# Attention and a two-layer block on one core: DMA transposes for one batch's q and k and another's x, and a reordered start

## The chip, the cores and the metric

The kernel runs on one core of a Trainium2 chip. The metric is device time in microseconds (us): the median of the runs shown, lower is better. A core has a matrix engine (PE; its weight loads, PEld, overlap the matmuls), a vector engine (DVE), a scalar engine (ACT), a general engine (POOL) and a sync engine (SP) that only issues DMAs here. Each engine takes its instructions strictly in the program's order and waits on semaphores for the others. ACT and POOL issue DMAs too, in line with their own work.

## The reference

Sliding-window causal attention over 8 batches, 8 heads, 576 positions, head size 64; its output, with the heads side by side, is the input x (4608 x 512) of a small two-layer block.

```python
scale = 1.0 / np.sqrt(D)
scores = scale * np.matmul(q, k.transpose(0, 1, 3, 2))
mask = (rel >= 0) & (rel < 64)              # rel = query position - key position
scores = np.where(mask, scores, -1e9)
attn = softmax(scores)
x = (attn @ v).transpose(0, 2, 1, 3).reshape(B * S, H * D)
h = x @ w_in                                # 512 -> 2048
g = h - np.tanh(h)
out = g @ w_out                             # 2048 -> 512, float32
```

## The kernel before

**Attention, by batch and pair of heads.** Heads r and r + 4 make a pair; g = 4 * batch + pair runs from 0 to 31. The 576 positions are nine windows of 64. For each pair q and k are loaded as rows, cast to bf16 (`cast`), transposed on PE in six pieces each against an identity (`tr`, L203) into PSUM, and copied to `qT` and `kT` (two buffers each, used in turn) by ACT or DVE. `qT` holds the two heads in separate halves of a zeroed tile, so one matmul per window gives both heads' scores (`scores`, L216), in three groups of three windows with one exponential on ACT each (L220). In batches 0 and 1 the mask is added by a second matmul (L219); later it is multiplied in by DVE (`masking`). `pv` (L230) multiplies by V with a column of ones, and `norm` divides on DVE into `xs`. For batches 0 to 2 the finished `xs` is transposed on PE (`x_tr`, L247) and copied out of PSUM into the chunk tiles `xT`; from batch 3 on, SP issues two DMA transposes straight from `xs` into `xT` (`x_dma`, L262).

**V.** V is loaded eight positions to a partition, moved into `vb` with the ones column in four pieces (`cast_v`), and spread by nine small DMAs (`keys_v`, L133) into the upper half of `vw`; the lower half is the same moved by one window (`shift_v`: DVE at L139 in batches 0 and 1, a DMA at L141 later). There is one `vb` and one V load tile, so a batch's V waits for the one before to be moved on.

**The two-layer block.** Nine chunks of 512 positions. The program runs in half steps h: at even h four matmuls (`hp_mm`, L273) make 128 columns of h for one chunk, ACT takes the tanh (L277), DVE subtracts (L283) into `gT`; at odd h four matmuls (`yp_mm`, L293) work on the output of the chunk before. One chunk takes 32 half steps; chunk c starts at h = 32c. `w_in` is loaded in three parts (512, 512 and 1024 columns: steps `w0`, `w1`, `w2`, needed at h = 0, 8 and 16), `w_out` in four (`o0` to `o3`).

**What sets the order.** Everything is placed by hand. Batches 0 to 2 are a script, `PLAN`, with an entry for a half step and an entry -1 for all that comes before the first; its letters are read by `play`: `q`/`r` load one pair's q/k, `Q`/`K`/`V` load a batch's q/k/v, `v` one pair's v, `a`/`b` cast q/k, `d` moves V into `vb`, `k` is a `keys_v` move, `z` the shift, `E`/`F` transpose q/k, `R` a group of scores, `P` a pair's `pv` and `norm`, `M` masking, `X` an x transpose, `w`/`o` weight loads, `i` the identity, `m` constants, `n` the mask; the last letters name the engine (p POOL, a ACT, v DVE, s SP). Batches 3 to 7 follow rules: pair g is transposed at half step a = 8g - 48 - (0, 2 or 4), scored at a + 5, a + 7 and a + 9, masked at a + 11, multiplied with V from a + 13, normalised at a + 15; loads and V's moves stand at fixed distances from s = 32b - (0, 2 or 4). For batch 7 that is a = 172, 180, 188, 196 and s = 220. From batch 4 on `pace` puts a tiny POOL copy that waits for a given step's `gT` ahead of each load, so that POOL doesn't issue it early.

SP issues, in program order, the `keys_v` moves, the shift, `x_dma` and the output rows (`y_out`); POOL issues all casting loads and does most casts.

Of the kernel before, what the change touches and what calls it, by code (L numbers as in the profile page):

```python
# [8 lines left out]
BF16 = mybir.dt.bfloat16  # L9
# [6 lines left out]
def kernel(  # L16
# [9 lines left out]
    nc = tc.nc  # L26
    B, H, S, D = q.shape
    NP = H // 2
    NJ = S // 64
    E, P = 6, S // 6  # L30
# [12 lines left out]
    const = ctx.enter_context(tc.tile_pool(name="const", bufs=1))  # L43
# [4 lines left out]
    sm_pool = ctx.enter_context(tc.tile_pool(name="sm", bufs=3))  # L48
    xt_pool = ctx.enter_context(tc.tile_pool(name="xt", bufs=3))
    g_pool = ctx.enter_context(tc.tile_pool(name="g", bufs=2))  # L50
    psum = ctx.enter_context(tc.tile_pool(name="psum", bufs=1, space=PSUM))


# [11 lines left out]
    NR, NPT = 2, 4  # L65
# [5 lines left out]
    PT = [const.tile([128, NJ, 128], BF16, name=f"pt{i}") for i in range(NPT)]  # L71
    kT = [const.tile([128, 64 + S], BF16, name=f"kt{i}") for i in range(NR)]
    qT = [const.tile([128, 2, S], BF16, name=f"qt{i}") for i in range(NR)]
    xs = [const.tile([128, NJ, NP, D], BF16, name=f"xs{i}") for i in range(2)]

    stage, rows, whole = {}, {}, {}
# [31 lines left out]
    def cast(g, n, eng=nc.gpsimd):  # L108
        t = row_pool.tile([P, E, 2, D], BF16, tag=n + "b", name=n + "b")
        move(eng, t.rearrange("p e h d -> p h e d"),  # L110
             stage.pop((g, n)).rearrange("p h (e d) -> p h e d", d=D))
        rows[g, n] = t

    def load_v(b, pr):
        if (b, "v") not in whole:
# [52 lines left out]
    def more_constants():  # L168
        nc.vector.memset(qT[1], 0.0)
        nc.vector.memset(kT[1][:, 0:64], 0.0)  # L170
        for i in range(2):
            nc.vector.memset(vw[i][0:64, 0], 0.0)

        for h in range(2):
            nc.gpsimd.memset(hide[:, h], 0.0)
            nc.gpsimd.affine_select(hide[:, h], hide[:, h], compare_op=ALU.is_ge, fill=-(2.0 ** 30),
                                    base=-1, pattern=[[-1, 64]], channel_multiplier=1)
            nc.gpsimd.affine_select(hide[:, h], hide[:, h], compare_op=ALU.is_ge, fill=-(2.0 ** 30),  # L180
                                    base=64, pattern=[[1, 64]], channel_multiplier=-1)

    def make_mask():
        nc.gpsimd.memset(seen, 1.0)
# [59 lines left out]
    def x_tr(b, half, w0, w1, bank, eng=nc.vector):  # L244
        tp = ps[:, bank, :].bitcast(BF16)[:, 0:640].rearrange("p (w t) -> p w t", t=128)
        for w in range(w0, w1):
            nc.tensor.transpose(tp[:, w - w0, :],  # L247
                                xs[b % 2][:, w, 2 * half:2 * half + 2, :].rearrange("p r d -> p (r d)"), ident)
        lo, hi = b * NJ + w0, b * NJ + w1
        while lo < hi:  # L250
            c = lo // WPC
            to = min(hi, (c + 1) * WPC)
            i0 = lo - b * NJ - w0
            move(eng, chunk_tile(c)[:, lo - c * WPC:to - c * WPC, half, :], tp[:, i0:i0 + to - lo])
            lo = to

    def x_dma(b):
        lo, hi = b * NJ, (b + 1) * NJ
        while lo < hi:
            c = lo // WPC  # L260
            to = min(hi, (c + 1) * WPC)
            nc.sync.dma_start(out=chunk_tile(c)[:, lo - c * WPC:to - c * WPC].rearrange("p w r t -> p (w r) t"),  # L262
                              in_=xs[b % 2][:, lo - b * NJ:to - b * NJ].rearrange("p w r d -> p (w r d)"),
                              transpose=True)
            lo = to
# [40 lines left out]
    def at(h, *fn):  # L306
        items.setdefault(h, []).append(fn)
# [8 lines left out]

    ENG = dict(p=nc.gpsimd, a=nc.scalar, v=nc.vector, s=nc.sync)

    def play(script):
        for step in script.split():
            what = step[0]
            n = [int(i, 36) for i in step[1:] if i not in "apvs"]
            eng = [ENG[i] for i in step[1:] if i in "apvs"]
            if what in "qr":
                load(*n, "q" if what == "q" else "k", *eng)
            elif what in "QK":
                load_all(*n, what.lower())
            elif what == "V":  # L330
                load_v_all(*n)
            elif what == "a":
                cast(*n, "q", *eng)
            elif what == "b":
                cast(*n, "k", *eng)
            elif what == "v":
                load_v(*n)
            elif what == "d":
                cast_v(*n, *eng)
            elif what == "k":  # L340
                keys_v(*n, *eng)
            elif what == "z":
                for j in (0, 4) if eng[0] is nc.vector else (0,):
                    shift_v(*n, j, j + 4 if eng[0] is nc.vector else NJ - 1, *eng)
            elif what == "E":
                tr(*n, "q", 3, *eng)
            elif what == "F":
                tr(*n, "k", 2 if n[0] < 2 * NP else 3, *eng)
            elif what == "R":
                scores(*n, (4, 0, 1)[n[1]] if n[0] < NP else 4)  # L350
            elif what == "P":
                for i in range(3):
                    pv(*n, i)
                norm(*n)
            elif what == "M":
                masking(*n)
            elif what == "X":
                b, half, part = n
                x_tr(b, half, 4 * part, 4 + 5 * part, 2 if part == 1 and b < 2 else 3, *eng)
            elif what == "w":  # L360
                load_w_in(*n)
            elif what == "o":
                load_w_out(*n)
            elif what == "i":
                make_ident()
            elif what == "n":
                make_mask()
            elif what == "m":
                more_constants()
# [1 line left out]

    PLAN = {
        -1: """
            v02 i q0a v00 a0v v01 d00a d02a d01v r2a m v03 q3p r1p d03p r0s q1a k03p k01a E0vv
            b0a k07p b2a q2p k00s b1v F0v k04p R01 V1 n k05s k02s k06a k08s R00 K1 a1v R02 Q1
            r3s E1vv w0 F1a F2a z0v R10 w1 a2p E2aa d12p d13a R11 R22 P0 d10a R12 R21 a3p d11p
            b3a E3aa k12s R20 P1 k13p F3v K2 a4p P2 k18s a7p k10s b7p Q2 k16s b4p w2 k11s R31
            R30 V2 a5p X000v a6p R32 P3 b6p o3 b5p X001a k15a X010v X011a o2 E4vv""",
        0: "a8p F4a",
        10: "R40 F5a b8p R42 b9p E5aa",  # L380
        12: "k14s R41 k17s z1v",
        15: """
            R50 a9p d21p E6av R51 F6v R52 P4 d23p R62 d22p bAa o1 F7v R61 d20p E7aa P5 R60 bBp
            o0""",
        16: "aAp R70 E8aa",
        20: "R72 X101a k23s X100v k21s k24s k27s P6",
        23: "F8a R71 F9a k22s P7 k25s k20s R80 k28p k26p E9av",
        24: "R82",
        27: "R81 z2s X110a",
        31: "R90 X111v M8 EAav",  # L390
        32: "R92",
        35: "FAa R91",
        36: "M9",
        41: "aBa P9 FBa",
        42: "RA1",
        45: "RA2 P8 EBaa RA0",
        50: "RB1 X201v RB2 MA X200a RB0 PA",
        56: "MB PB",
        60: "X210a",
        62: "X211a",  # L400
    }
    for h, script in PLAN.items():
        at(h, play, script)


    for g in range(3 * NP, B * NP):
        b, pr = divmod(g, NP)
        a = 8 * g - 48 - (0, 2, 4)[min(b - 3, 2)]
        s = 32 * b - (0, 2, 4)[min(b - 3, 2)]
        at(a - 7, cast, g, "q")  # L410
        at(a - 5, cast, g, "k")
        at(s - 72 + 5 * pr, cast_v, b, pr)
        at(a, tr, g, "q", 3, nc.scalar, nc.vector)
        at(a + 2, tr, g, "k", 3, nc.scalar)
        for i in range(3):
            at(a + 5 + 2 * i, scores, g, i, 4)
        at(a + 11, masking, g)
        for i in range(3):
            at(a + 13 + i, pv, g, i)
        at(a + 15, norm, g)  # L420
        if pr == NP - 1:
            at(a + 16, x_dma, b)
        for j in range(NJ):
            if pr == 0:
                at(s - 54 + j // 2, keys_v, b, j)
        if pr == 0:
            if b < 4:
                at(s - 78, load_v_all, b)
                at(s - 64, load_all, b, "q")
                at(s - 63, load_all, b, "k")  # L430
            else:
                for h, f in (s - 78, (load_v_all, b)), (s - 60, (load_all, b, "q")), (s - 64, (load_all, b, "k")):
                    at(h, pace, h)
                    at(h, *f)
            at(s - 47, shift_v, b, 0, NJ - 1)

    LAG = 16
    for h in range(min(items), 2 * (16 * NC + LAG) + 2):
        n = h // 2
# [42 lines left out]
```

## Time and profile before

| | |
|---|---|
| median of 5 runs | 353.88 us (351.64 to 354.59) |
| profiled execution, its own time | 354.85 us |
| its span (first to last instruction) | 353.1 us |
| first matmul of h = 0 | 40.47 us into the span |
| PE busy | 318.2 us, 90% |
| DVE, ACT, POOL busy | 203.2, 200.1, 106.7 us |
| mean granted PE clock | 0.995 |

"Busy" counts an engine's instructions from start to end; PE matmuls overlap, so the distance from one start to the next says more than their duration. In the lists below, a line of the timeline has the start, the time from the first start to the last end of its instructions, engine, source line, operation, what is written and read, and how many instructions; a bracket gives the idle time before it and what ended that. Issues of DMAs stand as work of the issuing queue (SPq, ACTq), on POOL as POOL's own.

### The profile page before, as it was taken

What the parts mean: (1) busy time and instruction counts of PE and PEld (TensorE: products, weight loads), DVE (VectorE), ACT (ScalarE), POOL (GpSimd) and SP (SyncE); (2) the same over time, 40 slices, a digit from 0 to 9 for tenths busy, and PEclk for the clock granted to TensorE, in tenths of its full rate; (3) what the DMA queues carried; (4) which work ended last, traced back from release to release, by engine and by line L of the source; (5) the groups of instructions that cost most, each with busy time, mean ns of one, the idle gap of its engine ahead of it and who ended that gap; (6) DMA issues with size and microseconds to landing.
All of it is one profiled execution on the core that took longest, in us unless ns stands there. A gap on an engine that the chain in (4) does not pass through costs nothing.

```text
span 353.1 us, 5838 instructions
## 1 busy us (share of the span) xinstructions
PE 318.2 (90%) x2208; PEld 184.5 (52%) x2239; DVE 203.2 (58%) x319; ACT 200.1 (57%) x360; POOL 106.7 (30%) x151
## 2 busy tenths in 40 slices
PE   0357778999899999999999999999999999999995
PEld 0347546655556555555555555555555444444442
DVE  2435568865676666666666767776676333334400
ACT  3446478965756666566566666666664444444411
POOL 6928526406407430832462246330000000000000
PEclk9999899999999999999999999999999999999999
DMA  7999993759864766976686678544001400010021
GB/s 141 179 196 211 219 192 55 151 99 178 176 125 68 133 109 143 161 138 117 115 160 135 133 148 128 126 101 97 32 31 40 119 30 32 30 59 32 30 84 66
DMA packets 43692, 39.85 MB, mean 113 GB/s; under 512 B 15408, under 2 KB 37552, under 8 KB 43280
## 3 DMA queue, kind: packets, MB, share of 16 engines
q0 software_dynamic: 20368, 18.02, 34.8%
q1 hardware_dynamic: 22456, 20.37, 21.4%
q10 hardware_dynamic: 840, 1.08, 1.1%
q8 instruction: 17, 0.28, 0.3%
q14 instruction: 11, 0.09, 0.1%
HBM read 36.70 MB, written 9.44 MB: 131 GB/s over the span
## 4 chain that ended last, share of the span: by engine, by line
PE 77%; DVE 7%; ACT 6%; DMA 3%; issue 1%; POOL 1%; ACTq 0%; POOLq 0%
PE ps L293 33%; PE ps L273 32%; PE ps L216 4%; PE ps L230 4%; DMA vall<-in_v_dram 3%; PE ps L203 3%; DVE xs L241 3%; DVE gT L283 2%; ACT pt L220 2%; ACT th L277 2%; ACT qt L80 1%; PE ps L219 1%; DVE qt L82 1%; DVE pt L224 1%; POOL vw L133 1%
## 5 line engine op out<-in xcount | busy, mean ns | idle before, releaser
L283 DVE TENSOR_TENSOR gT<-ps,th 128x512 bf16<-128x512 f32 x144 | 99.4, 692 | 91.7 <-ACT th L277 89.0
L273 PE MATMUL ps<-xT,wi 128*128 128x512 bf16 x576 | 148.5, 381 | 1.9 <-DVE gT L283 1.1
L293 PE MATMUL ps<-w_out_sb,gT 128*128 128x512 bf16 x545 | 140.1, 379 | 1.8 <-ACT ysb L298 0.2
L277 ACT ACTIVATE th<-ps 128x512 f32<-128x512 f32 x144 | 86.0, 598 | 79.3 <-PE ps L273 78.8
L273 PEld LDWEIGHTS <-wi 128*128 128x128 bf16 x576 | 61.1, 114 | 47.5 <-issue 3.6
L293 PEld LDWEIGHTS <-gT 128*128 128x128 bf16 x576 | 53.6, 98 | 53.8 <-issue 0.5
L220 ACT ACTIVATE pt<-ps 128x384 bf16<-128x384 f32 x96 | 47.0, 491 | 37.2 <-PE ps L216 29.9
L241 DVE TENSOR_TENSOR xs<-ps,rc 64x576 bf16<-64x576 f32 x64 | 48.3, 755 | 1.5
L82 POOL COPY vb<-vall 72x1024 bf16<-72x1024 bf16 x27 | 28.3, 1057 | 51.9 <-DMA vall<-in_v_dram 42.5
L216 PE MATMUL ps<-qt,kt 128*128 128x128 bf16 x288 | 37.5, 230 | 7.2 <-ACT pt L220 4.5
L82 POOL COPY qb<-qall 96x768 bf16<-96x768 bf16 x29 | 24.1, 832 | 38.4 <-DMA qall<-in_q_dram 27.8
L230 PE MATMUL ps<-vw,pt 128*128 128x130 bf16 x288 | 30.1, 229 | 4.6 <-DVE vw L139 2.0
L230 PEld LDWEIGHTS <-pt 128*128 128x128 bf16 x288 | 23.1, 103 | 20.0 <-issue 3.0
L82 DVE COPY qt<-ps 64x576 bf16<-64x576 bf16 x29 | 21.9, 757 | 16.9 <-ACT qt L80 13.6
L216 PEld LDWEIGHTS <-kt 128*128 128x128 bf16 x288 | 25.2, 104 | 11.0 <-DVE kt L82 2.2
L298 ACT ACTIVATE ysb<-ps 128x512 f32<-128x512 f32 x36 | 21.5, 598 | 14.7 <-PE ps L293 14.7
L82 POOL COPY kb<-kall 96x768 bf16<-96x768 bf16 x27 | 22.9, 847 | 9.9 <-PE ps L203 6.6
L80 ACT ACTIVATE qt<-ps 64x576 bf16<-64x576 bf16 x35 | 22.3, 637 | 0.9 <-PE ps L203 0.9
L203 PE MATMUL ps<-ident,kb 96*128 96x96 bf16 x192 | 14.6, 217 | 7.5 <-ACT kb L80 5.7
L203 PE MATMUL ps<-ident,qb 96*128 96x96 bf16 x192 | 14.7, 217 | 6.4 <-DVE qb L82 6.1
L80 ACT ACTIVATE kt<-ps 128x576 bf16<-128x576 bf16 x28 | 18.1, 648 | 2.7 <-PE ps L203 2.6
L203 PEld LDWEIGHTS <-kb 96*128 96x128 bf16 x192 | 12.3, 104 | 13.5 <-ACT kb L80 5.9
(49 smaller groups left out, 131.5 us busy)
## 6 DMA issues: line engine op xcount, KB each, us to landing
out_dram<-ysb SPq DMA_DIRECT2D x36, 256.0 KB
vw<-vb SPq DMA_DIRECT2D x63, 65.0 KB
vall<-in_v_dram POOLq DMA_DIRECT2D x7, 576.0 KB, 12.3
kall<-in_k_dram POOLq DMA_DIRECT2D x7, 576.0 KB, 6.9
qall<-in_q_dram POOLq DMA_DIRECT2D x7, 576.0 KB, 8.7
vw<-vw SPq DMA_DIRECT2D x6, 520.0 KB
w_out_sb<-in_moe_w_out_dram POOLq DMA_DIRECT2D x4, 512.0 KB, 10.9
wi<-in_moe_w_in_dram POOLq DMA_DIRECT2D x2, 512.0 KB, 19.1
```

Source lines behind the costliest of these rows:

```text
L80: nc.scalar.activation(o, i, ACT.Copy)
L82: eng.tensor_copy(o, i)
L203: nc.tensor.transpose(tp[:, e, :], src[:, e, :], ident[:P, :P])
L216: nc.tensor.matmul(sp[:, i, :], kT[g % NR][:, 64 * j:64 * j + 128], qT[g % NR][:, :, 64 * j:64 * j + 64], start=True, stop=g >= 2 * NP)
L220: nc.scalar.activation(PT[g % NPT][:, 3 * grp:3 * grp + 3, :], sp, ACT.Exp, scale=scale)
L230: nc.tensor.matmul(ps[:, 5 + grp, 130 * i:130 * i + 130], PT[g % NPT][:, j, :], vw[b % 2][:, j, 2 * pr:2 * pr + 2, :], start=True, stop=True)
L241: nc.vector.tensor_tensor(xo[r, :, :, pr, :], ov[r, :, :, h, 0:D], rc[r].to_broadcast([64, 3, 3, 64]), ALU.mult)
L273: nc.tensor.matmul(hp, w_in_tile(ki, m), chunk_tile(c)[:, :, ki % 2, 64 * (ki // 2):64 * (ki // 2) + 64], start=(ki == 0), stop=(ki == 3))
L277: nc.scalar.activation(th, hp, ACT.Tanh)
L283: nc.vector.tensor_tensor(gT[c][:, m, :], hp, th, ALU.subtract)
L293: nc.tensor.matmul(yp, gT[c][:, m, s * 128:(s + 1) * 128], w_out_sb[:, m, :], start=(m == 0), stop=(m == M - 1))
L298: nc.scalar.activation(ysb, ps[:, yp_bank(c, s), :], ACT.Copy)
```

## The change

```diff
+    dram = ctx.enter_context(tc.tile_pool(name="dram", bufs=2, space=bass.MemoryType.DRAM))
+    qz = [const.tile([P, 2, E, 128], BF16, name=f"qz{i}") for i in range(2)]
...
+    def cast_q(g):
+        i = stage.pop((g, "q")).rearrange("p h (e d) -> p h e d", d=D)
+        for h in range(2):
+            nc.gpsimd.tensor_copy(qz[g % 2][:, h, :, 64 * h:64 * h + 64], i[:, h])
+
+    def bounce(g, n):
+        if n == "q":
+            t = dram.tile([2, S, 128], BF16, tag="q", name="qd")
+            nc.sync.dma_start(out=t.rearrange("h (p e) c -> p h (e c)", e=E),
+                              in_=qz[g % 2].rearrange("p h e c -> p h (e c)"))
+        else:
+            t = dram.tile([S, 128], BF16, tag="k", name="kd")
+            nc.sync.dma_start(out=t.rearrange("(p e) c -> p (e c)", e=E),
+                              in_=rows.pop((g, "k")).rearrange("p e h d -> p (e h d)"))
+        rows[g, n + "d"] = t
+
+    def tr_dma(g, n):
+        t = rows.pop((g, n + "d"))
+        if n == "q":
+            nc.sync.dma_start(out=qT[g % NR].rearrange("c h s -> c (h s)"),
+                              in_=t.rearrange("h s c -> (h s) c"), transpose=True)
+        else:
+            nc.sync.dma_start(out=kT[g % NR][:, 64:], in_=t, transpose=True)
...
+            elif what == "Y":
+                x_dma(*n)
...
     PLAN = {
         -1: """
-            v02 i q0a v00 a0v v01 d00a d02a d01v r2a m v03 q3p r1p d03p r0s q1a k03p k01a E0vv
-            b0a k07p b2a q2p k00s b1v F0v k04p R01 V1 n k05s k02s k06a k08s R00 K1 a1v R02 Q1
-            r3s E1vv w0 F1a F2a z0v R10 w1 a2p E2aa d12p d13a R11 R22 P0 d10a R12 R21 a3p d11p
-            b3a E3aa k12s R20 P1 k13p F3v K2 a4p P2 k18s a7p k10s b7p Q2 k16s b4p w2 k11s R31
-            R30 V2 a5p X000v a6p R32 P3 b6p o3 b5p X001a k15a X010v X011a o2 E4vv""",
+            r2a q0s v02 v03 v00 v01 a0v r0s d00a d01v d02a m i r1p q3p q1a d03p b0a k01s a1v
+            k08s k00s b1p k03p n k02s F0a E0av R01 R02 q2p E1av k07p V1 k06a a3p k04p b2v K1 a2a
+            R00 F1v k05s r3a E2aa F2a Q1 w0 R10 z0v d12p R22 d13p R12 P0 R11 E3aa R20 P1 d10p
+            b3a d11p k12s k13p R21 k16p a7p w1 F3a b4a P2 a4p R30 R31 X000v Q2 R32 P3 b7a X001a
+            k10s K2 b5p a6p F4a k18s w2 X010v k11s k17s b6p a5p b9p V2 k15a X011v E4vv""",
...
-        50: "RB1 X201v RB2 MA X200a RB0 PA",
+        50: "MA RB2 RB0 PA RB1",
         56: "MB PB",
-        60: "X210a",
-        62: "X211a",
+        58: "Y2",
     }
...
+    def more_zeros(i):
+        nc.gpsimd.memset(qz[i], 0.0)
...
+    for i in range(2):
+        at(66 + 2 * i, more_zeros, i)
...
-        at(a - 7, cast, g, "q")
-        at(a - 5, cast, g, "k")
         at(s - 72 + 5 * pr, cast_v, b, pr)
-        at(a, tr, g, "q", 3, nc.scalar, nc.vector)
-        at(a + 2, tr, g, "k", 3, nc.scalar)
+        if b < 7:
+            at(a - 7, cast, g, "q")
+            at(a, tr, g, "q", 3, nc.scalar, nc.vector)
+        else:
+            at(a - 14, cast_q, g)
+            at(a - 12, bounce, g, "q")
+            at(a - 6, tr_dma, g, "q")
+        if b < 7:
+            at(a - 5, cast, g, "k")
+            at(a + 2, tr, g, "k", 3, nc.scalar)
+        else:
+            at(a - 13, cast, g, "k")
+            at(a - 11, bounce, g, "k")
+            at(a - 5, tr_dma, g, "k")
...
-                for h, f in (s - 78, (load_v_all, b)), (s - 60, (load_all, b, "q")), (s - 64, (load_all, b, "k")):
+                hq, hk = s - (60 if b < 7 else 68), s - (64 if b < 7 else 72)
+                for h, f in (s - 78, (load_v_all, b)), (hq, (load_all, b, "q")), (hk, (load_all, b, "k")):
```

The entries of `PLAN` for h = 0 to 45 are reordered in the same way. Of those that the prediction speaks of: F4 goes from h = 0 into the start, F5 from ACT to DVE, F7 from DVE to ACT, and R40 from h = 10 to 15. In batch 7 q and k of a pair now go from POOL's cast to a DRAM tile (two DMAs) and from there by two DMA transposes into `qT` and `kT`; q's rows carry zeros in the other head's half, so the transposes write the whole of `qT`. Batch 2's x goes by `x_dma` at h = 58 in place of eighteen PE transposes.

## The prediction
> **What bounds the kernel now.** I read the page's 40 slices first, then PE's timeline in the steady part, then the chain of waits and the engines' timelines in the first 41 us.
>
> ```profile
> PE   0357778999899999999999999999999999999995
> DMA  7999993759864766976686678544001400010021
> L203 PE MATMUL ps<-ident,kb 96*128 96x96 bf16 x192 | 14.6, 217 | 7.5 <-ACT kb L80 5.7
> ```
>
> PE is full from about 90 us to the end, and starved for the first 40, where the DMA engines are full instead. So a PE instruction taken out late is worth its whole step, one taken out early little, and the start is a matter of what arrives when. One transpose has a mean of 217 ns, but its step must be read from starts:
>
> ```profile
> 239.68 0.41 PE L203 MATMUL ps<-ident,kb 96*128 96x96 bf16 x6
> 239.94 1.03 PE L293 MATMUL ps<-w_out_sb,gT 128*128 128x512 bf16 x4
> 240.80 1.03 PE L273 MATMUL ps<-xT,wi 128*128 128x512 bf16 x4
> ...
> 249.25 1.03 PE L273 MATMUL ps<-xT,wi 128*128 128x512 bf16 x4
> ```
>
> Six 96-column transposes hold PE 239.94 - 239.68 = 0.26 us. A pair's eight half steps take 249.25 - 240.80 = 8.45 us with no idle bracket; the same eight without attention take 293.76 - 286.85 = 6.91 us later in that timeline.
>
> **The change, last batch.** Out: per pair 12 transposes. 4 pairs x 2 x 0.26 = 2.08 us of full PE, plus three copies per pair (ACT 0.63 and 0.65, DVE 0.76) on engines that are 60 to 70% busy there. Call it -2.0. The DMA work that replaces it is hidden if it is in time, and two queues decide that.
>
> POOL first. These are its rows for batch 7 now:
>
> ```profile
> 207.21 1.05 POOL L82 COPY vb<-vall 72x1024 bf16<-72x1024 bf16 x1 [6.80 <-DMA vall<-in_v_dram]
> ...
> 216.44 0.77 POOL L99 DMA_DIRECT2D qall<-in_q_dram  x1 [0.30 <-issue]
> ...
> 226.08 0.83 POOL L82 COPY qb<-qall 96x768 bf16<-96x768 bf16 x1 [7.80 <-DMA qall<-in_q_dram]
> ```
>
> The q load moves from h = 160 to 152 (by 8.45 us), but it stands behind the V copy that ends at 208.2, a k load and two casts (0.78 + 0.84 + 0.83), two paced copies and their gaps (about 0.9): issue near 211.6, not 208. Landing took 9.5 us from issue here, 6.1 for k: 217.7 to 221.1. Behind the new `cast_q` of pair 28, which waits for it, stand one V copy and the cast of k of pair 27: 0.83 (two halves of one cast) + 1.05 + 0.83 = 2.7, so k of pair 27 is ready at 220.4 to 223.8. PE transposes it at 222.78 now. Loss 0 to 1.0; I take 0.5.
>
> SP second. Per pair it gains two writes (0.53 each by the shift's row) and two DMA transposes. A transpose costs SP 1.18 to 1.57 us to issue (L262, 2 to 16 blocks), and for q and k I take 1.4 and 1.3. Four pairs: 4 x 3.8 = 15 us in 30 us of an SP that now issues about 11 us there, and each transpose waits for its write. The transposes of pair 28 and V's nine moves (0.65 each) share SP from h = 166: by adding up, pair 29's k transpose is issued near 237, lands 3 to 4.4 us later (L262: issue at 271.62, DMA share back to 0 by 277.6, two transposes, 18 blocks) at 240 to 241.4, and is due at 242.70. Transposes out of DRAM are not in this trace: at best as from SBUF (3.0), at worst as the slowest load there (9.5), nearer the first for 9 and 4.5 blocks of 256-byte rows. At worst pair 28 and 29 would stand 1 to 5 us late once, after which SP has caught up. I take 0.1. Last batch: -2.0 + 0.5 + 0.1 = -1.4 (bounds -2.1 to +3.5).
>
> The Trainium skill speaks to the size of the first term: "TensorE: Matmul & The Clock Gate", Part 4, gives about 275 ns for one PE transpose inside a kernel; by it 48 + 18 of them would be 18 us. The steps above show 43 ns, since the next instruction starts long before the last one's end, and the sum goes by the steps. Against the change stands the skill's "DMA: Bandwidth & Descriptors", Rules for kernel authors: a DMA that reads what another DMA wrote must wait on that one's semaphore before it is issued, whatever the queue. That is SP's waiting here; the trace has it at the V shift (SP waited 20.0 us in 7 such waits, 2.9 each), and the walk above contains it.
>
> **Batch 2's x.** Out: 18 transposes.
>
> ```profile
> 107.34 0.39 PE L247 MATMUL ps<-ident,xs 128*128 128x128 bf16 x4
> 107.56 1.03 PE L293 MATMUL ps<-w_out_sb,gT 128*128 128x512 bf16 x4
> ```
>
> Four hold PE 0.22 us, five 0.28. The nine at h = 60 and 62 are in full PE: -0.5. The nine at h = 50 lie between groups of scores that wait for ACT anyway (PE idles 0.62 and 0.36 us there for an exponential); in the new order P of pair 10 (0.51 us) fills one such wait: -0.5. ACT and DVE lose 2.5 us of copies. The new transposes wait for the last `norm`, which ends at 104.63; 12 blocks should land after a 1.4 us issue and 2 us of transfer, 108.2; chunk 2 starts at 111.28, sooner by what is saved. Hidden with 1 to 2 us to spare; if DMA is shared with a V load as in the 12.3 us row, up to 5 late. -1.0 (bounds -1.5 to +1.5).
>
> **The start.** What sets h = 0 now:
>
> ```profile
> 13.02 12.30 DMA vall<-in_v_dram
> 25.39 1.09 ACT vb L80
> 26.51 0.88 ACT pt L220 x2
> ...
> 31.00 0.23 DVE rc L237
> ```
>
> ACT waits for batch 1's V and holds back the exponentials of pairs 1 and 2 behind it. Those V moves go to POOL, so this stand is gone. What remains is V of batch 0:
>
> ```profile
> 24.67 0.70 DVE L139 COPY vw<-vw 64x2080 bf16<-64x2080 bf16 x1 [2.40 <-DMA vw<-vb]
> 26.05 0.22 DVE L237 RECIPROCAL rc<-ps 128x9 f32<-128x9 f32 x1 [0.68 <-PE ps L230]
> ```
>
> From pair 0's norm (26.05) on, four norms of 1.78 and three `pv` of 1.2 in between (32.84 to 34.01), then 1.42 to h = 0 (39.05 to 40.47): 7.1 + 3.6 + 1.4 = 12.1, so 38.2 instead of 40.47 would be possible. But the shift now comes later. `k06` was issued by ACT at 15.76 and landed by 24.67 (8.9 us); in the new order it stands on ACT behind the first copies and exponentials, and those behind q of pair 1: issued near 8.0 (V's first landings 7.3 to 7.6), landing after 6.3 us (k: 7.33 to 13.60), then DVE's cast 0.57 and half copy 0.76, two groups of scores 1.3, the next transposes 0.5: `k06` at 17.6, landed 26.5. Shift at 26.5, norm at 27.9, h = 0 at 40.0, plus 0.25 because both last copies of x are now DVE's: 40.3, -0.2. Bounds: shift still at 24.67 (-2.0); `k06` as slow as V's load, 12.3: 29.9, h = 0 at 43.7 (+3.2). After h = 0 ACT loses three copies' worth and gains one (F4 and F5 out, F7 in, 0.65 each) in a stretch that PE spends waiting for exponentials (49.9 to 60.3), and one more group of scores moves into it (+0.5): -0.3 (-1 to +1). Start: -0.5 (-3.0 to +4.2).
>
> **Sum.** -1.4 - 1.0 - 0.5 = -2.9 on a span of 353.1, which has 1.75 us outside it in its run of 354.85. Taken off the median: 353.88 - 2.9 = 351.0.
>
> **Rivals.**
>
> A. The start gains too. `k06` lands with the others as before; POOL's moves of 65 KB landed in 4.4 to 7.1 us. For it: ACT's stand is certainly gone. Then the start is at its lower bound: 353.88 - 1.4 - 1.0 - 3.0 = 348.5.
>
> B. The start gives the gain back: V's low half late, the start at +3.2 - 0.3 = +2.9: 353.88 - 1.4 - 1.0 + 2.9 = 354.4. For it: DMA full to 10 tenths until 55 us, so whatever is issued later lands later.
>
> C. The last batch gives its gain back: POOL's cast behind the q load (1.0) and SP's line (1 late): 353.88 - 1.5 = 352.4. Against: SP catches up.
>
> D. Slower: `w1`. It was issued at 17.23; now it stands on POOL behind the four V copies of batch 1 (V lands 25.3 to 26.5, 4 x 1.05), two moves (1.2), two casts: issue near 33.5. It is due at h = 8, 46.24 now. The three parts of `w_in` took 16.0 to 20.6 us to land; with these, 49.5 to 54.1, 3.3 to 7.9 late, mid 5.6: 353.88 - 2.9 + 5.6 = 356.6. It decides from a landing at 51. Against: most of those 16 to 20 us was waiting behind loads that will be done at 33.5 (`w1` followed `w0` by 3.7 us).
>
> **Numbers.** Forecast 0.41 (349.5 to 352.1), A 0.16, B 0.15, C 0.10, D 0.18. About 0.5% is what a measurement here can tell from nothing: 352.1 to 355.6. Faster 0.57, same 0.25 (B, C), slower 0.18 (D). The range holds A to nearly D: 347.5 to 356.5.
>
> **What would show it.** Right: pairs' eight half steps down from 8.45 to about 7.95 us in batch 7, no PE idle before its scores; none at chunk 2; h = 0 at 39 to 41; ACT without a 3 us idle before its V copies. Wrong: PE idle before h = 8 on `wi` (D), at pair 27's k transposes (C), before L230 of pair 0 beyond 26 us (B).

## The result, and the profile after

| | before | after |
|---|---|---|
| median | 354.03 us (79 runs) | 352.73 us (44 runs, 349.56 to 357.13) |
| ratio after / before | | 0.9947, 95% interval 0.9933 to 0.9961 |
| profiled execution, its own time | 354.85 us | 355.65 us |
| its span | 353.1 us | 353.9 us |

The change is faster by 0.53% (0.39 to 0.67%), about 1.9 us where 2.9 were forecast. The ratio leaves out each run that is more than 1.5% above the fastest of its kernel, ten of the 44 after and one of the 79 before; over all runs the medians are 1.3 us apart. The changed kernel is also less even: its runs spread over 7.6 us, those of the kernel before over 5.4 (351.64 to 357.03). The profiled execution of the changed kernel is one of its longer ones, longer than that of the kernel before, so it is read by its parts and not by its total, and a second execution of the same kernel ("after, 2nd") stands beside it.

The table is made from the first matmul of a half step, taken from the traces (L273 before, now L304). All numbers are us.

| stretch | before | after | after, 2nd |
|---|---|---|---|
| span's start to h = 0 | 40.47 | 38.91 | 37.91 |
| span's start to h = 8 | 46.24 | 43.97 | 43.13 |
| h = 8 to 40 | 35.01 | 35.06 | 35.12 |
| h = 40 to 48 | 9.02 | 12.76 | 8.78 |
| h = 48 to 64 (batch 2's x) | 21.01 | 20.03 | 20.01 |
| h = 64 to 160 | 104.16 | 104.17 | 104.16 |
| h = 160 to 216 (last batch) | 57.60 | 57.78 | 57.24 |
| h = 216 to the end | 80.10 | 80.14 | 80.14 |

So in these two executions the start gained 2.3 and 3.1 us, x gained its 1.0, and the last batch, which was to bring the most, brought nothing in the one execution and 0.4 in the other. In between a loss of 3.7 us stands in one execution and not in the other.

The page's slices of the changed kernel:

```profile
PE   0267788897899999999999999998999999999995
PEclk9999999998999999999999999999999999999999
DMA  8699999959767867976586698559821400010021
```

A slice is 8.8 us. PE has two holes that it didn't have: the tenth slice (80 to 88 us, where the granted clock dips too) and the 28th (239 to 248 us), in the last batch. The one in the last batch comes first. PE's timeline there:

```profile
232.36 1.03 PE L304 MATMUL ps<-xT,wi 128*128 128x512 bf16 x4
...
240.28 1.03 PE L304 MATMUL ps<-xT,wi 128*128 128x512 bf16 x4
...
242.60 0.27 PE L261 MATMUL ps<-vw,pt 128*128 128x130 bf16 x2 [0.37 <-DMA vw<-vw]
244.13 0.34 PE L247 MATMUL ps<-qt,kt 128*128 128x128 bf16 x3 [1.26 <-DMA kt<-kd]
...
250.17 1.03 PE L304 MATMUL ps<-xT,wi 128*128 128x512 bf16 x4
```

The first eight half steps take 240.28 - 232.36 = 7.92 us instead of 8.45: the transposes are out, as forecast. The next eight take 9.89, since PE waits for V's shift (`vw`) and then for the transposed k (`kt`) of pair 29. SP's queue, which issues both:

```profile
234.70 0.45 SPq L130 DMA_DIRECT2D kd<-kb  x1
235.19 1.09 SPq L161 DMA_DIRECT2D vw<-vb  x1
237.66 0.52 SPq L169 DMA_DIRECT2D vw<-vw  x1
238.29 3.21 SPq L137 DMA_TRANSPOSE qt<-qd  x1
241.54 1.26 SPq L140 DMA_TRANSPOSE kt<-kd  x1
```

The shift has to wait until the last of V's moves has landed, and both transposes of pair 29 stand behind it (SP stands idle from 236.28 to 237.66); q's then holds SP for 3.21 us. k's is issued at 241.54 and serves PE at 244.13.

The earlier hole, at batch 2's V: POOL's, SP's and PE's timelines of the changed kernel, then PE's of the kernel before.

```profile
66.93 0.86 POOL L151 DMA_DIRECT2D vall<-in_v_dram  x1
67.78 1.14 POOL L161 DMA_DIRECT2D vw<-vb  x2
...
70.43 0.58 POOL L161 DMA_DIRECT2D vw<-vb  x1
```

```profile
78.12 0.53 SPq L169 DMA_DIRECT2D vw<-vw  x1
```

```profile
83.14 1.04 PE L261 MATMUL ps<-vw,pt 128*128 128x130 bf16 x8 [2.16 <-DMA vw<-vw]
...
84.78 1.91 PE L304 MATMUL ps<-xT,wi 128*128 128x512 bf16 x4
```

```profile
82.97 0.75 PE L230 MATMUL ps<-vw,pt 128*128 128x130 bf16 x9
```

Three of batch 2's V moves are issued just behind the load of batch 3's V. By their semaphores they land when that load does (77.4), at 77.6 to 77.9, 7 to 10 us after their issue; the shift follows at 78.12 and lands at 83.1, and PE has waited 2.16 us for it, where the kernel before had no wait. After it four matmuls hold PE for 1.7 us instead of 0.86.

The start: DVE's timeline of the kernel before, then DVE's and PE's of the changed one.

```profile
31.00 0.22 DVE L237 RECIPROCAL rc<-ps 128x9 f32<-128x9 f32 x1 [3.17 <-PE ps L230]
```

```profile
26.45 0.70 DVE L167 COPY vw<-vw 64x2080 bf16<-64x2080 bf16 x1 [4.39 <-DMA vw<-vb]
27.83 0.22 DVE L268 RECIPROCAL rc<-ps 128x9 f32<-128x9 f32 x1 [0.68 <-PE ps L261]
...
30.83 0.22 DVE L268 RECIPROCAL rc<-ps 128x9 f32<-128x9 f32 x1 [1.23 <-PE ps L261]
```

```profile
29.66 1.14 PE L261 MATMUL ps<-vw,pt 128*128 128x130 bf16 x9
...
32.67 0.67 PE L261 MATMUL ps<-vw,pt 128*128 128x130 bf16 x9 [0.47 <-DVE xs L272]
...
38.91 2.00 PE L304 MATMUL ps<-xT,wi 128*128 128x512 bf16 x8
...
43.97 1.89 PE L304 MATMUL ps<-xT,wi 128*128 128x512 bf16 x8 [0.55 <-DVE gT L314]
```

The V shift of batch 0 is later (24.67 before) and pair 0's norm too, but pair 1's norm, at 31.00 before with 3.17 us of idle DVE ahead, is at 30.83. h = 0 starts at 38.91, and PE's idle time before h = 8 ends on `gT`, not on the weights of `w1`.

### The profile page after: what moved, and what is told of

The parts are those of the page before. It is cut to its first block, busy times and chain, and to the rows that moved or that the text cites. A ratio compares the mean times of both kernels' runs of the same rounds, so it can differ in the third digit from the quotient of the medians.

```text
span 353.9 us, 5709 instructions
## 1 busy us (share of the span) xinstructions
PE 315.3 (89%) x2142; PEld 180.2 (51%) x2173; DVE 198.3 (56%) x314; ACT 193.1 (55%) x347; POOL 112.2 (32%) x160
## 4 chain that ended last, share of the span: by engine, by line
PE 71%; DMA 10%; DVE 6%; ACT 5%; POOL 4%; issue 2%; SPq 0%; ACTq 0%; DVEq 0%; POOLq 0%
PE ps L324 31%; PE ps L304 29%; DMA vw<-vb 5%; PE ps L261 4%; PE ps L247 4%; DVE xs L272 3%; PE ps L234 2%; DMA vall<-in_v_dram 2%; DVE gT L314 2%; DMA kt<-kd 2%; ACT th L308 1%; DMA vw<-vw 1%; ACT pt L251 1%; ACT qt L82 1%; DVE qt L84 1%
## 5 line engine op out<-in xcount | busy, mean ns | idle before, releaser
L304 PE MATMUL ps<-xT,wi 128*128 128x512 bf16 x576 | 148.2, 381 | 1.8 <-DVE gT L314 1.7
L304 PEld LDWEIGHTS <-wi 128*128 128x128 bf16 x576 | 61.2, 114 | 47.8 <-issue 3.7
L84 POOL COPY vb<-vall 72x1024 bf16<-72x1024 bf16 x29 | 30.8, 1074 | 54.5 <-DMA vall<-in_v_dram 40.0
L84 DVE COPY qt<-ps 64x576 bf16<-64x576 bf16 x24 | 18.2, 759 | 18.8 <-ACT qt L82 18.8
L84 POOL COPY kb<-kall 96x768 bf16<-96x768 bf16 x26 | 21.7, 838 | 13.0 <-DMA kall<-in_k_dram 12.6
L84 POOL COPY qb<-qall 96x768 bf16<-96x768 bf16 x24 | 20.0, 834 | 16.4 <-DMA qall<-in_q_dram 16.4
L82 ACT ACTIVATE qt<-ps 64x576 bf16<-64x576 bf16 x32 | 20.4, 637 | 1.2 <-PE ps L234 0.9
L82 ACT ACTIVATE kt<-ps 128x576 bf16<-128x576 bf16 x25 | 16.2, 648 | 4.4 <-PE ps L234 4.2
L255 DVE TENSOR_TENSOR pt<-pt,ps 128x1152 bf16<-128x1152 bf16 x24 | 17.9, 745 | 0.0
L234 PE MATMUL ps<-ident,kb 96*128 96x96 bf16 x168 | 12.9, 218 | 2.0 <-ACT xT L82 0.9
L234 PEld LDWEIGHTS <-kb 96*128 96x128 bf16 x168 | 10.8, 105 | 6.8 <-issue 2.4
```

What stands on the lines that cost most here:

```text
L82: nc.scalar.activation(o, i, ACT.Copy)
L84: eng.tensor_copy(o, i)
L234: nc.tensor.transpose(tp[:, e, :], src[:, e, :], ident[:P, :P])
L304: nc.tensor.matmul(hp, w_in_tile(ki, m), chunk_tile(c)[:, :, ki % 2, 64 * (ki // 2):64 * (ki // 2) + 64], start=(ki == 0), stop=(ki == 3))
```

## The experiments

Twelve entries, ten other kernels and the changed one twice more, in three groups; each group ran on one chip with its own runs of the kernel before, so ratios are compared within a group first. The last two columns are lengths from the profiled execution of each.

| kernel | ratio, 95% interval | h = 40 to 48 | h = 160 to 216 |
|---|---|---|---|
| **group 1** (before 354.12) | | | |
| after, 2nd | 0.9967, 0.9937 to 0.9996 | 8.78 | 57.24 |
| last batch undone | 0.9960, 0.9939 to 0.9982 | 8.78 | 57.59 |
| batch 2's V moves on SP | 0.9923, 0.9893 to 0.9954 | 9.30 | 57.50 |
| last batch's V moves on POOL | 0.9903, 0.9864 to 0.9942 | 11.84 | 55.66 |
| **group 2** (before 354.57) | | | |
| x alone | 0.9969, 0.9941 to 0.9997 | 8.94 | 57.60 |
| new start alone | 0.9937, 0.9914 to 0.9960 | 8.78 | 57.60 |
| V moves ahead of V's load | 0.9972, 0.9944 to 0.9999 | 8.78 | 57.10 |
| the same, last batch's V moves on POOL | 0.9886, 0.9855 to 0.9917 | 8.78 | 55.82 |
| **group 3** (before 354.35) | | | |
| last batch alone | 1.0042, 1.0013 to 1.0072 | 8.95 | 60.22 |
| last batch alone, its V moves on POOL | 0.9981, 0.9956 to 1.0005 | 8.94 | 56.11 |
| V moves of batch 2 on SP, of the last on POOL | 0.9916, 0.9885 to 0.9946 | 9.19 | 55.47 |
| after, 3rd | 0.9947, 0.9921 to 0.9973 | 8.78 | 59.62 |

### The three parts, each alone

Batch 2's x alone, put into the kernel before:

```diff
+            elif what == "Y":
+                x_dma(*n)
...
-        50: "RB1 X201v RB2 MA X200a RB0 PA",
+        50: "MA RB2 RB0 PA RB1",
         56: "MB PB",
-        60: "X210a",
-        62: "X211a",
+        58: "Y2",
```

> The kernel before with one part of the change: batch 2's x by DMA transposes at h = 58, and the order of the groups around h = 50 that goes with it. Theory: half steps 48 to 64 take 20.0 us instead of 21.0, no PE wait at chunk 2, and all of it stays to the end: 1.0 us faster, ratio 0.996 to 0.998. Rival (the transposes land late or crowd the loads of batch 3): 0 or slower.

The time fell by 0.31% (0.03 to 0.59), 1.1 us of 354.57; h = 48 to 64 took 19.99 us instead of 21.01. Chunk 2 starts without a wait. PE's timeline of this kernel at that place:

```profile
110.53 0.33 PE L216 MATMUL ps<-qt,kt 128*128 128x128 bf16 x3
110.70 1.03 PE L273 MATMUL ps<-xT,wi 128*128 128x512 bf16 x4
```

No bracket stands at 110.70, so the transposes were in time. The -1.0 of the forecast is what the trace shows, and the time agrees with it within a wide interval.

The new start alone, the changed kernel without the other two parts (`b < 7` becomes `b < 8` in both places, and `more_zeros` is out):

```diff
-        50: "MA RB2 RB0 PA RB1",
+        50: "RB1 X201v RB2 MA X200a RB0 PA",
         56: "MB PB",
-        58: "Y2",
+        60: "X210a",
+        62: "X211a",
...
-        if b < 7:
+        if b < 8:
...
-                hq, hk = s - (60 if b < 7 else 68), s - (64 if b < 7 else 72)
+                hq, hk = s - 60, s - 64
```

> The kernel before with the new script for the start and h = 0 to 45 alone; x of batch 2 and batch 7 as before. Theory: h = 0 comes 0.8 to 2.6 us earlier, h = 40 about 1.4 to 3 us earlier, and in executions where batch 2's V lands late the wait for its shift near h = 41 takes 0.5 to 4 us back: on the median 0.5 to 1.5 us faster, ratio 0.996 to 0.9985. Rival (nothing is given back at V): 2 us faster or more, 0.9945 or less.

-0.63% (0.40 to 0.86), 2.2 us. This is the rival's side of the expectation, and the largest gain of the three, where the forecast had put the smallest. Its profiled execution had no wait at half step 41.

The last batch alone, the kernel before with the new code for batch 7 and the old `PLAN` (the main lines):

```diff
+            at(a - 14, cast_q, g)
+            at(a - 12, bounce, g, "q")
+            at(a - 6, tr_dma, g, "q")
...
+            at(a - 13, cast, g, "k")
+            at(a - 11, bounce, g, "k")
+            at(a - 5, tr_dma, g, "k")
...
+                hq, hk = s - (60 if b < 7 else 68), s - (64 if b < 7 else 72)
```

> The kernel before with the last batch's part alone, V's moves of that batch still issued by SP. Theory (SP's line gives the gain back): a pair without waits takes 7.92 us for its eight half steps instead of 8.45, 4 x 0.53 = 2.1 out, and about 1.4 to 2.2 back in waits of pv on the V shift and of the scores on k; h = 160 to 216 in 56.7 to 57.6 us against 57.60 before, ratio 0.997 to 1.000. Rival (the last batch gives its forecast 1.4 and what is missing in the changed kernel was lost at batch 2's V shift alone): h = 160 to 216 in about 56.2 us, ratio 0.995 to 0.996, and no wait of PE on kt.

Worse than both had it: +0.42% (0.13 to 0.72), 1.5 us slower, and 60.22 us for a stretch that took 57.60. PE's timeline shows the two waits again, longer, and something behind them:

```profile
242.56 0.27 PE L261 MATMUL ps<-vw,pt 128*128 128x130 bf16 x2 [0.94 <-DMA vw<-vw]
244.41 0.50 PE L247 MATMUL ps<-qt,kt 128*128 128x128 bf16 x3 [1.57 <-DMA kt<-kd]
244.71 1.91 PE L304 MATMUL ps<-xT,wi 128*128 128x512 bf16 x4
...
248.20 1.03 PE L304 MATMUL ps<-xT,wi 128*128 128x512 bf16 x4
```

The four matmuls at 244.71 take twice their time, until about 247.9. The table by windows shows it (each stretch's bounds and length, PE's busy time and instructions, the granted clock, the DMA share and GB/s):

```profile
240.00:245.00 5.00, 2.49 (x15) 0.88 0.91 219
245.00:250.00 5.00, 5.00 (x27) 0.77 0.92 201
250.00:255.00 5.00, 5.00 (x34) 1.00 0.82 219
```

So a wait of 2.5 us costs 4.2: pair 29's eight half steps take 12.14 us and not 7.92, the waits and then some three us at half rate.

The three parts add up: -0.31 - 0.63 + 0.42 = -0.52%, against -0.53% for the whole. In us that is -1.1 - 2.2 + 1.5 = -1.8. Each part is known to about 1 us only, so that they meet the whole this closely is partly chance.

### The last batch: undone, and with a free SP

> The changed kernel once more, as the base of this group and for a second profile. Theory: the new start brings the half steps to h = 40 about 2 us earlier, and the matmuls of pairs 8 and 9 with V, just behind it, then wait for batch 2's shift of V: 2.3 us of PE idle near 81 us and a first group of matmuls at 1.9 us instead of 0.86. If that wait belongs to every execution, it is here again, 1.5 to 3 us; if it was an accident of the one profiled execution, it is under 0.5 us. Time 350.5 to 353.5, ratio 0.990 to 0.998.

The second run of the changed kernel gave 353.45 us and 0.9967; its trace has no wait at batch 2's V, so that wait belongs to some executions only, and again 1.19 us on `kt` for pair 29.

The last batch undone, all else as in the changed kernel (the two lines with `b < 8` and `s - 60, s - 64` of the diff above):

> Batch 7's q and k transposed on PE again, everything else as changed. Theory: in the profile of the changed kernel batch 7 gained nothing, the 2.1 us of PE steps saved were spent on waits for pair 29's k transpose, for V's shift and for pair 30; then this is 0 to 0.5 us from the changed kernel. Rival (the saving stands, the waits belong to one execution): 1.5 to 2.1 us slower than the changed kernel.

352.68 us and 0.9960, against 0.9967 with the last batch's part: taking out the part that was to bring the most changes the time by less than the intervals can tell. Inside the changed kernel the last batch's part thus cost +0.2 us (-1.1 to +1.5 by the two intervals), beside the +1.5 that it cost alone. Which of the two is nearer the truth these runs don't settle; the forecast's -1.4 lies outside both.

V's moves of the last batch issued by POOL instead of SP, a single line of the changed kernel:

```diff
-                at(s - 54 + j // 2, keys_v, b, j)
+                at(s - 54 + j // 2, keys_v, b, j, nc.sync if b < 7 else nc.gpsimd)
```

> The changed kernel with batch 7's nine V moves issued by POOL instead of SP. Theory: SP was too full between 223 and 243 us (transposes, writes and nine V moves in turn), so pair 29's k transpose was issued at 241.5 for a use at 242.8; without the V moves it is issued before 236, the waits of 0.4, 1.3 and 0.2 us are gone, 1.5 to 2 us faster than the changed kernel. Rival: the transposes wait for their writes to DRAM or for the DMA engines, not for SP; then under 0.5 us.

351.26 us, 0.9903 beside 0.9967 for the changed kernel in the same group. SP's timeline, then PE's:

```profile
233.98 0.52 SPq L169 DMA_DIRECT2D vw<-vw  x1
234.61 2.76 SPq L137 DMA_TRANSPOSE qt<-qd  x1
237.42 1.27 SPq L140 DMA_TRANSPOSE kt<-kd  x1
```

```profile
239.50 1.03 PE L304 MATMUL ps<-xT,wi 128*128 128x512 bf16 x4
...
241.58 0.34 PE L247 MATMUL ps<-qt,kt 128*128 128x128 bf16 x3
```

k's transpose of pair 29 is issued 2.1 us before h = 184 (239.50), where SP with V's moves issued it 1.3 us after (241.54 against 240.28). The brackets before `pv` and the scores are gone, and the stretch takes 55.66 us, 1.9 less than with PE transposes. It is in time by very little: by its semaphore k lands at 241.53, 4.1 us after its issue, and PE uses it at 241.58. Measured from h = 184 the issue came 3.3 us earlier than with V's moves on SP, the landing only 1.8 (241.53 - 239.50 against 244.09 - 240.28). The same line in the kernel with the last batch alone:

> The same with the last batch's nine V moves issued by POOL instead of SP. Theory: no wait on kt or on V's shift in the last batch, h = 160 to 216 in 55.5 to 55.9 us, ratio 0.994 to 0.995 (-1.8 to -2.1 us), clearly under that of the last batch's part with V's moves on SP. Rival (POOL's cast behind the q load is what costs): POOL's extra nine issues make k of pair 27 later, PE waits at its transposes, and the ratio is the same as with SP or above.

0.9981 beside 1.0042, 56.11 us beside 60.22, with one wait of 0.28 us on `kt` left. Against the kernel before that is 0.7 us, less than the 1.8 expected: the interval (0.9956 to 1.0005) just excludes 1.8 us and doesn't exclude none. In the profiled execution the stretch itself gained 1.5. At pair 27's k transposes PE had no wait, so POOL's nine more issues cost nothing there. The two comparisons, 0.9967 to 0.9903 and 1.0042 to 0.9981, are both some 2.2 us for the same line.

The third run of the changed kernel, in the same group:

> The changed kernel once more, unchanged, as the base for the other three runs. Theory: 0.993 to 0.997 of before; in the trace the wait of pv at half step 41 lies between 0 and 3 us, following when batch 2's V load lands, and the waits on kt and on V's shift in the last batch (together 1.4 to 2.2 us) are there again. Rival (the last batch's waits were accidents of one execution): they are absent or under 0.5 us in sum.

The waits of the last batch are there again (0.81 on `vw` and 1.36 on `kt`), and behind them the slow matmuls (pair 29: 12.08 us). At half step 41 PE didn't wait.

### Batch 2's V

The three moves of batch 2's V that POOL issued late, given to SP, and then, in another kernel, left on POOL but put ahead of the load of batch 3's V:

```diff
-        23: "F8a R71 F9a k21p k22p aBp R80 P7 E9av k26s bBp k24p R82",
+        23: "F8a R71 F9a k21s k22s aBp R80 P7 E9av k26s bBp k24s R82",
```

```diff
-        16: "E8aa k23p aAp R70",
+        16: "E8aa k23p k21p k22p k24p aAp R70",
-        23: "F8a R71 F9a k21p k22p aBp R80 P7 E9av k26s bBp k24p R82",
+        23: "F8a R71 F9a aBp R80 P7 E9av k26s bBp R82",
```

> The changed kernel with three small V moves of batch 2 (k21, k22, k24) issued by SP instead of POOL, where they stand behind the load of batch 3's V. Theory: these moves land near 78 us because of that load, the shift waits for them and lands at 83; on SP they land by 75 or 76, the shift by 81, and the PE wait near 81 us falls from 2.3 to under 0.5 us together with the slow first group behind it: 2 to 3.3 us faster than the changed kernel, ratio to before near 0.986 to 0.989. Rival: the shift's own transfer beside the V load is the slow part; then under 0.7 us.

> The changed kernel with POOL's three late V moves of batch 2 issued ahead of the load of batch 3's V instead of behind it. Theory: in POOL's queue they no longer stand behind that load, and SP's moves share with it for less time; the shift is issued near 73 to 76 us instead of 74.6 to 79, lands before h = 41 in every execution, no PE wait there: 0.7 to 1.5 us faster than the changed kernel on the median, and a narrower spread (no runs above 354.5). Rival: SP's moves also wait for the DMA engines until the load is done, as when three moves went to SP (shift still at 77.45); then 0 to 0.5 us.

On SP the shift was issued at 77.45 in its execution, still when batch 3's load had ended, and a wait of 0.36 us was left (9.30 us). Ahead of the load, POOL's and SP's timelines read:

```profile
63.11 2.31 POOL L161 DMA_DIRECT2D vw<-vb  x4 [0.30 <-POOL vb L84]
...
66.14 0.88 POOL L151 DMA_DIRECT2D vall<-in_v_dram  x1
```

```profile
71.44 0.54 SPq L169 DMA_DIRECT2D vw<-vw  x1
```

The moves land by 71.3 instead of 77.9 and the shift is issued 6.7 us earlier than in the changed kernel: it is the load ahead of them that held the moves. But the shift now runs beside that load and by its semaphore lands with it, at 78.92 (the load at 79.11), 7.5 us after its issue and not 5.0. The changed kernel's second execution, which had no wait either, has it landed at 78.83, so the missing wait isn't shown to come from this edit. In the time nothing shows. The first kernel's ratio is 0.9923, the second's 0.9972 in a group that had no run of the changed kernel; both intervals overlap that of the changed kernel. The narrower spread that was expected of the second didn't come: four of its twelve runs are above 354.5. In the changed kernel's executions the wait was 2.2, 0 and 0 us (and 2.9 with the last batch's moves on POOL, 0 with the last batch undone), so it is a cost of some executions, and its share in the median isn't settled.

### The edits together

> Both mends: POOL's V moves of batch 2 ahead of the load of batch 3's V, and batch 7's V moves on POOL. Theory: the two gains add, 2.0 us at batch 7 and 0.7 to 1.5 at batch 2: 2.7 to 3.5 us faster than the changed kernel, 348.5 to 350, ratio to before 0.985 to 0.989. Rival (what is gained at one is lost at the next wait): no better than the mend of batch 7 alone, 0.990.

> The changed kernel with V's moves of batch 2 that POOL issued (k21, k22, k24) given to SP, and the last batch's V moves given to POOL. Theory: the two edits touch different places and add: the last batch in 55.6 to 55.9 us, the wait of pv at half step 41 between 0 and 0.6 us, ratio 0.986 to 0.990, 349.2 to 350.6 us. Rival (only the last batch's edit counts in the time, the wait at half step 41 is mostly an accident of the profiled executions): ratio 0.990 to 0.992, the same as with the last batch's edit alone.

With V's moves ahead of the load and the last batch's on POOL: 350.55 us, 0.9886, inside what was expected. With batch 2's moves on SP and the last batch's on POOL: 351.03 us, 0.9916, and 0.24 us of wait at half step 41; that is the rival's ratio, not the theory's. Beside 0.9903 for the last batch's edit alone the three intervals overlap: that edit is shown to pay, and the one for batch 2's V is shown to move the V moves and not the time. All three beat the kernel before by about 1%; the changed kernel's 0.9947, from all groups, lies 0.3 to 0.6% above them.

## Why the prediction was right, and where it wasn't

The direction was right and 1.9 of 2.9 us came, but not from where the forecast had them: two terms were wrong in opposite directions, and that the total came near is luck. What happened is most of rival A's larger start and rival C's last batch at once.

- **Transposes of the last batch, -2.08.** Right: eight half steps went from 8.45 to 7.92 us, a saving of 0.53 for each pair, 2.1 for four.
- **SP's line, +0.1.** This is the step that failed. It gave SP's issues by adding up durations, and found k of pair 29 issued near 237 and landed by 240 to 241.4. It was issued at 241.54. The forecast had named the V shift's wait and held it for contained in its walk. Three things, some 4.9 us together, make that up. Both transposes of pair 29 stand behind that shift, which waits for the landing of V's last move (SP idle for 1.4 us, 236.28 to 237.66); the nine moves held SP for 7.6 us and not 9 x 0.65 = 5.9; and q's transpose held it for 3.21 and not 1.4. In all ten executions with this part q's transpose of pair 29 took 2.75 to 3.30 us, those of pairs 28 and 31 1.2 to 1.3; why isn't shown. That k would land 3 to 4.4 us after its issue was nearly right (2.6 here, up to 4.3 with V's moves on POOL), and so was that SP catches up afterwards. The late landings, V's shift and k, cost 1.6 to 2.1 us in four executions (eight half steps in 9.5 to 10.0 us for 7.92) and 4.2 in the two where the clock fell. The whole term was -1.4; alone it measured +1.5 (0.5 to 2.5), inside the changed kernel +0.2.
- **POOL's cast behind the q load, +0.5.** Over-sized in the changed kernel. The load was issued at 211.68 (forecast 211.6), landed by 219.4, and the k casts began at 221.36, inside the bounds; PE had no wait at pair 27's k transposes in the changed kernel, and 0.38 us with the last batch alone (its eight half steps 8.99 us for 8.45). POOL's timeline of the changed kernel, then PE's:

```profile
211.68 0.77 POOL L101 DMA_DIRECT2D qall<-in_q_dram  x1
...
219.47 0.96 POOL L120 COPY qz<-qall 96x384 bf16<-96x384 bf16 x2 [5.21 <-DMA qall<-in_q_dram]
...
221.36 1.60 POOL L84 COPY kb<-kall 96x768 bf16<-96x768 bf16 x2
```

```profile
223.32 0.42 PE L234 MATMUL ps<-ident,kb 96*128 96x96 bf16 x6
```

- **Batch 2's x, -1.0.** Right in mechanism and size: 1.0 us out of h = 48 to 64 in nine of the ten executions that had it (0.7 in the other), and no wait at chunk 2.
- **The start, -0.5.** That pair 1's norm would follow pair 0's was right, and the size wrong. The shift came at 26.45 for a forecast of 26.5, but by another path, and the agreement is luck. The forecast had `k06` land last; ACT issued it at 18.58 (forecast 17.6) and by its semaphore it landed at 25.44. The shift waited for `k04`, which POOL issued behind the load of batch 1's V (lines below) and which landed at 26.37, that load at 25.61: what happened to batch 2's moves too. From the norm on the forecast laid the old durations end to end: 12.1 us to h = 0. It was 38.91 - 27.83 = 11.1, because a `pv` from 32 us on takes 0.67 us, not the 1.14 of the one at 29.66. All matmuls quicken there: two of 128 columns start 107 ns apart until 31 us and 56 ns apart from 33 on. In the kernel before, the `pv` at 36.11 still takes 1.13. The trace's record of the granted clock begins at that change: at 31.98 in this execution, at 35.6 to 36.8 in the four with the old start, at 28.3 to 32.1 in nine of the ten with the new one. The forecast had no term for it. Two more terms weren't in the sum either: h = 0 to 8 took 5.06 us instead of 5.77, and h = 32 to 40 took 7.55 instead of 8.35, since chunk 1's last copies to `xT` are no longer late; h = 8 to 32 gave 0.85 back. Over the profiled executions, four with the old start and ten with the new, the median of h = 40 is 81.5 and 79.6. No run takes the start's parts one by one, so what each is worth is read from the traces alone. POOL's timeline of the changed kernel:

```profile
14.82 0.84 POOL L151 DMA_DIRECT2D vall<-in_v_dram  x1
...
16.43 0.59 POOL L161 DMA_DIRECT2D vw<-vb  x1
```

- **A wait that the forecast hadn't listed: `pv` at half step 41.** The forecast followed the V moves of batches 0 and 1 and not those of batch 2, which went behind a load on POOL. In the kernel before, the shift's landing and PE's arrival were within 0.1 us of each other (both near 83); a start 2 us earlier turns that into a wait whenever the load isn't earlier by as much: it was issued 0.5 us earlier than before (66.93 for 67.44) in the execution with the wait, 3.0 us earlier (64.42) in the second, which had none. The question of what is late next, once the start is quicker, was not put.
- **`w1` (rival D).** Fell. It was issued at 33.3 (forecast 33.5) and landed by its semaphore at 41.1 to 44.8 in the ten executions, 8 to 11 us after its issue, not the 20.6 of before, when it had stood behind other loads. In one execution PE waited 0.72 us for it.

## What to carry to other kernels

A queue's time isn't the sum of durations seen elsewhere: here the issues themselves took longer (some 3.5 us), and a DMA that waited for the landing of another held up all that was queued behind it (1.4 us). What is due next shouldn't stand behind either; moving nine small issues to another engine brought 2.2 us here, as much as the transposes that were taken out. When work is taken off the critical path early, look at the next thing that had been just in time. And check a forecast by its parts: here an error of +2.9 us in one term and one of -1.7 in another left a total that looked nearly right, and a landing time was right to 0.05 us by another DMA than the one forecast.

## What the runs showed of the hardware

The clock of TensorE made part of what differs between executions of one program. The table by windows, of the kernel before and then of the changed one:

```profile
38.00:40.00 2.00, 0.68 (x9) 0.95 1.25 223
40.00:42.00 2.00, 1.97 (x10) 0.50 1.21 217
42.00:44.00 2.00, 2.00 (x12) 0.69 1.16 217
```

```profile
38.00:40.00 2.00, 1.92 (x19) 1.00 0.85 114
40.00:42.00 2.00, 1.39 (x8) 1.00 1.15 183
```

Before, PE was busy for a third of the time ahead of h = 0 and began the two-layer block at half its clock; all four executions with the old start have such a stretch, from about 40 to 43 us, and the new start has it in four of ten. With it h = 0 to 8 takes some 5.75 us, without it 5.05: 0.7 us of the start's gain, present or not. Those of the last batch followed two waits of together 2.2 and 2.5 us, but together 1.6 us in another execution brought none; at half step 41 one wait of 2.16 us brought it, and one of 2.88 us in another kernel did not.

The traces say when it falls. The fourteen profiled executions have eleven half-rate stretches ahead of their last 20 us. Each lasted 3.41 us, and within one execution all changes of the granted clock lie on one grid of 3.41 us: in the changed kernel the record begins at 31.98, and the next changes are at 83.18, 15 such steps later, and at 86.59. The tables below have two steps of that grid, then two of the kernel with the last batch's V moves on POOL, where PE waited from 81.17 to 84.05 without losing the clock:

```profile
79.77:83.18 3.41, 1.25 (x8) 1.00 0.88 191
83.18:86.59 3.41, 3.41 (x21) 0.50 1.10 150
```

```profile
79.75:83.16 3.41, 1.41 (x8) 1.00 0.89 168
83.16:86.57 3.41, 2.47 (x24) 1.00 0.89 158
```

The grid cut the longer wait in two. In the step ahead of each of the eleven stretches PE was busy for 37 to 56% of the time; of the other steps at full rate, some 1200, four were at 56% or under (41, 51 and twice 56). So it goes by how idle PE is within one step, and half of a step was enough; between 41 and 56% the busy share alone doesn't decide. The Trainium skill, "TensorE: Matmul & The Clock Gate", Part 1, describes a free-running window of about 3.4 us that halves the clock after an idle window and restores it after a busy one. The length and the grid agree with it; that a whole window has to be idle doesn't, since waits well under 3.4 us were enough here.

Small DMAs issued behind a large load (65 KB behind 576 KB) took as long as the load: the three on POOL 7 to 10 us in the changed kernel, ending within 0.6 us of it. Issuing them from another queue didn't help (shift at 77.45). Issuing them 1.3 to 3 us before the load did (71.44), but then the shift itself, 520 KB, ran beside the load and landed with it.
